# A streaming layer-scale kernel: x's 4 head rows move from the first load to the last, and the tail is cut 56 + 4

## The chip, the cores and the metric

The kernel runs on one core of one Trainium2 chip. The metric is the device time of one execution in microseconds (us), taken as the median of several runs. Smaller is better.

## The reference

The inputs x and y are 1024 x 16 x 512 in bf16, and gamma has 512 elements. The whole computation is one line:

```python
def reference(x, y, gamma):
    return x + gamma * y
```

Flattened, x, y and the output each have 16384 rows of 512 elements, so 1 KB to a row and 16.78 MB to a tensor. Two tensors are read and one is written: 50.33 MB in all, with one multiplication and one addition for each element.

## The kernel before

There is no loop over tiles at run time: four lists, written out by hand at the top of the file, say which transfer and which vector operation is issued in which order.

The 16384 rows are spread over 128 partitions, 128 rows to a partition. `BLOCKS = [4, 64, 60]` cuts them into three blocks of DRAM; inside a block each partition owns consecutive rows. A transfer is written `('y', 4, 68)`: rows 4 to 67 of every partition, 64 rows of 1 KB. This text calls it y64, the first four rows y4, and so on; a store is s64, s4 or s60. `y_sb` holds all 128 rows of y; the products and the sums are written over it in place, and the stores read it. `x_sb` is smaller, 76 rows, and is used twice: the fourth number of an x load is the row of `x_sb` where it lands, so that later loads of x overwrite rows that an addition has already used.

- `SP` (line 12) is what the SyncE queue issues, in order; `ACT` (line 20) is what the ScalarE queue issues: before, it loads x4, then gamma, and then it does all stores. The two queues feed two DMA rings (q1 for SP and q10 for ACT in the profile), and the same 16 DMA engines serve both. Every 128-partition transfer gives each DMA engine 8 partitions; the trace records one packet for each partition of a transfer, and one 4-byte packet for each engine that signals its semaphore.
- `ring` (line 113) issues a list. A load of x waits for the additions whose rows it overwrites (`frees`, line 102). The first `EARLY` transfers of each list are put ahead of everything else in the program. The rest waits (`HOLD`, line 147) until y4 has landed.
- `RELEASE` names the load whose landing lets the stores start. TensorE waits for it (line 157) and then signals ScalarE (`s_go`) and VectorE (`s_rel`).
- `PIECES = [8, 16, 44, 52, 8]` cuts the 128 rows for VectorE; `DVE` lists its work: `('m', c)` multiplies piece c by gamma (line 180), `('a', c)` adds x to it (line 189). A store waits for the additions of the rows it writes.
- gamma arrives as one row, is spread to 128 partitions by a matmul with a row of ones (line 152) and copied to SBUF (line 154).

The order of work around the change, before: SP issues y4 and y64 at once while ACT issues x4; after y4 has landed, SP issues x64 and y60; after the addition of piece 2 it issues x52 (rows 68 to 119), and after the addition of piece 0 it issues x8 (rows 120 to 127). When x52 has landed, the stores go out on ACT's ring: s64, s4, s60.

Of the kernel before, what the change touches and what calls it, by code (L numbers as in the profile page):

```python
# [5 lines left out]

BLOCKS = [4, 64, 60]

PIECES = [8, 16, 44, 52, 8]


SP = [
    ('y', 0, 4),
    ('y', 4, 68),
    ('x', 4, 68, 4),
    ('y', 68, 128),
    ('x', 68, 120, 24),
    ('x', 120, 128, 0),
]
ACT = [('x', 0, 4, 0), ('g',), ('s', 4, 68), ('s', 0, 4), ('s', 68, 128)]  # L20

EARLY = (2, 1)

HOLD, AHEAD = ('y', 0, 4), (2, 1)

RELEASE = ('x', 68, 120, 24)

DVE = [('m', 0), ('m', 1), ('m', 2), ('a', 2), ('a', 0), ('a', 1), ('m', 3), ('m', 4), ('a', 3), ('a', 4)]
MULT, ADD = mybir.AluOpType.mult, mybir.AluOpType.add


def _take(sem, n, eng):


    return eng.wait_ge(sem, n).then_inc(sem, -n)  # L35


def kernel(
# [18 lines left out]
    rows = N // P  # L57
    n = len(PIECES)
    assert sum(PIECES) == rows
    starts = [sum(PIECES[:c]) for c in range(n + 1)]  # L60
    dt = xf.dtype
# [13 lines left out]
    y_sb = nc.alloc_sbuf_tensor("y_sb", [P, rows, D], dt).ap()  # L75
    x_loads = [w for w in ACT + SP if w[0] == "x"]
    y_loads = [w for w in SP + ACT if w[0] == "y"]
    stores = [w for w in SP + ACT if w[0] == "s"]
    for loads in (x_loads, y_loads, stores):
# [9 lines left out]
    s_add, s_go, s_rel, s_end, s_out = sem("s_add"), sem("s_go"), sem("s_rel"), sem("s_end"), sem("s_out")  # L89
    added = [a for kind, *a in DVE if kind == "a"]  # L90
    order = {a[0]: k for k, a in enumerate(added)}

    def meets(a, b, c, d):
        return a < d and c < b
# [4 lines left out]
    def x_at(row):  # L99
        return next(w[3] + row - w[1] for w in x_loads if w[1] <= row < w[2])  # L100
# [12 lines left out]
    def ring(eng, what, n_early, n_ahead):  # L113

        known, went = 0, False
        for k, w in enumerate(what):
            kind = w[0]
            if k == n_ahead:
                _take(s_held[eng], 1, eng)
            need = frees(w) if kind == "x" else pieces_of(w[1], w[2]) + list(w[3:]) if kind == "s" else []  # L120
            need = max((order[c] + 1 for c in need), default=0)
            if kind == "s" and not went:
                _take(s_go, 1, eng)
                went = True
            if need > known:
                eng.wait_ge(s_add, need)
                known = need
            if kind == "g":
                i = eng.dma_start(out=gamma_row, in_=gamma.unsqueeze(0)).then_inc(s_gamma, 16)
            elif kind == "x":  # L130
                to = x_sb[:, w[3] : w[3] + w[2] - w[1], :]
                i = eng.dma_start(out=to, in_=rows_of(xf, w[1], w[2])).then_inc(s_load[w], 16)
            elif kind == "y":
                r = slice(w[1], w[2])
                i = eng.dma_start(out=y_sb[:, r, :], in_=rows_of(yf, w[1], w[2])).then_inc(s_load[w], 16)
            else:
                r = slice(w[1], w[2])
                i = eng.dma_start(out=rows_of(of, w[1], w[2]), in_=y_sb[:, r, :]).then_inc(s_out, 16)
            if k < n_early:
                early.append(i.ins)  # L140

    ring(nc.sync, SP, EARLY[0], AHEAD[0])
    ring(nc.scalar, ACT, EARLY[1], AHEAD[1])

# [11 lines left out]

    _take(s_load[RELEASE], 16, nc.tensor)
    nc.tensor.sem_inc(s_go, 1)
# [4 lines left out]
    def need(loads, c):  # L163
        for w in loads:
            if w not in landed and meets(starts[c], starts[c + 1], w[1], w[2]):
                if w == RELEASE:
                    _take(s_rel, 1, nc.vector)
                elif w == HOLD:
                    _take(s_held[nc.vector], 1, nc.vector)
                else:  # L170
                    _take(s_load[w], 16, nc.vector)
                landed.add(w)

    for kind, *args in DVE:
        c = args[0]
        yt = y_sb[:, starts[c] : starts[c + 1], :]
        if kind == "m":
            need(y_loads, c)
            g = gamma_sb[:, None, :].to_broadcast([P, PIECES[c], D])
            nc.vector.tensor_tensor(out=yt, in0=yt, in1=g, op=MULT).then_inc(s_dve, 1)  # L180
            open_mults += 1
        else:
# [4 lines left out]
            at = x_at(starts[c])  # L187
            xt = x_sb[:, at : at + PIECES[c], :]
            nc.vector.tensor_tensor(out=yt, in0=xt, in1=yt, op=ADD).then_inc(s_add, 1)  # L189
# [44 lines left out]
```

## Time and profile before

| What | Value |
|---|---|
| Time, median of 3 runs | 119.62 us (119.55 to 119.73) |
| Span of the profiled execution, first to last instruction | 118.2 us |
| Time outside the span (median less span) | 1.4 us |
| DMA traffic | 50.33 MB, 1442 packets, mean 426 GB/s |
| DMA rings: share of the time of 16 engines | q1 64.8%, q10 33.9% |
| VectorE busy | 70.1 us, 12 instructions |
| TensorE busy | 0.6 us, one matmul |

The profile states the span of its execution but no separate time for it, so the span is set beside the median of the timed runs. The two shares of the DMA rings add up to 98.7% of the span: the sixteen DMA engines carry packets almost from the first instruction to the last. VectorE's work is spread over 59% of the span. The profile page gives for each DMA issue its size and its time to landing, for instance 57.3 us for y60, which is issued early and waits behind other transfers in its ring.

### The profile page before, as it was taken

To read this page: it belongs to the slowest core of one execution; us is meant where nothing else is said; L and a number is where in the kernel's file an instruction comes from. 1 tells how busy PE (TensorE), PEld (TensorE's weight loads), DVE (VectorE), ACT (ScalarE), POOL (GpSimd) and SP (SyncE) were. 2 spreads that over 40 slices of the span, in tenths; PEclk is the share of its full clock that TensorE was granted. 3 is DMA by queue.
4 is the path that set the end of the run, shared out by engine and by line. 5 is a ranking of instruction groups with operands and counts; after the bars stand their busy time and mean duration, and the time that the engine had idled before them with its cause. 6 is when DMAs were issued, how large, how long until landed. Compare 5 with 4: busy or idle time off the path is not lost. (4 is left out here: it accounts for less than half of the span.)

```text
span 118.2 us, 91 instructions
## 1 busy us (share of the span) xinstructions
PE 0.6 (0%) x1; PEld 0.1 (0%) x1; DVE 70.1 (59%) x12; POOL 0.2 (0%) x4
## 2 busy tenths in 40 slices
PE   0000100000000000000000000000000000000000
PEld 0000000000000000000000000000000000000000
DVE  0000200089999969999999999999999900000000
POOL 0000000000000000000000000000000000000000
DMA  6999889988899879879969696898899889799793
GB/s 248 461 666 399 355 355 399 665 355 355 355 599 466 355 333 624 374 333 499 499 288 576 288 576 288 360 637 355 355 576 488 355 355 510 333 582 416 333 499 166
DMA packets 1442, 50.33 MB, mean 426 GB/s; under 512 B 161, under 2 KB 162, under 8 KB 546
## 3 DMA queue, kind: packets, MB, share of 16 engines
q1 hardware_dynamic: 864, 33.03, 64.8%
q10 hardware_dynamic: 578, 17.30, 33.9%
HBM read 33.56 MB, written 16.78 MB: 426 GB/s over the span
## 5 line engine op out<-in xcount | busy, mean ns | idle before, releaser
L180 DVE TENSOR_TENSOR y_sb<-y_sb,gamma_sb 128x4096 bf16<-128x4096 bf16 (+3 forms) x5 | 34.7, 6981 | 10.9 <-DVEq L35 10.9
L189 DVE TENSOR_TENSOR y_sb<-x_sb,y_sb 128x4096 bf16<-128x4096 bf16 (+3 forms) x5 | 34.7, 6981 | 1.2 <-DVEq L35 1.1
L154 DVE CAST gamma_sb<-gamma_ps 128x512 bf16<-128x512 f32 x1 | 0.7, 692 | 10.2 <-DVEq L35 10.2
L146 DVE MEMSET ones_row<- 1x128 bf16 x1 | 0.2, 165 | 2.0 <-PEq L51 2.0
L152 PE MATMUL gamma_ps<-gamma_row,ones_row 1*128 1x512 bf16 x1 | 0.6, 581 | 11.6 <-PEq L35 11.6
L152 PEld LDWEIGHTS gamma_ps<-gamma_row,ones_row 1*128 1x128 bf16 x1 | 0.1, 101 | 11.6 <-issue 11.6
L218 POOL MEMSET const-bfloat16-1.0<- 128x1 bf16 x1 | 0.1, 101 | 0.0
L218 POOL MEMSET const-uint8-127<- 128x1 uint8 x1 | 0.1, 101 | 0.0
L218 POOL MEMSET const-float32-0.0<- 128x1 f32 x1 | 0.1, 98 | 0.2 <-issue 0.2
L218 POOL MEMSET const-float32-1.0<- 128x1 f32 x1 | 0.1, 98 | 0.0
## 6 DMA issues: line engine op xcount, KB each, us to landing
y_sb<-in_y_dram SPq DMA_DIRECT2D x1, 7680.0 KB, 57.3
out_dram<-y_sb ACTq DMA_DIRECT2D x1, 7680.0 KB, 23.8
x_sb<-in_x_dram SPq DMA_DIRECT2D x1, 6656.0 KB, 21.7
x_sb<-in_x_dram SPq DMA_DIRECT2D x1, 1024.0 KB, 22.0
y_sb<-in_y_dram SPq DMA_DIRECT2D x1, 512.0 KB, 3.4
x_sb<-in_x_dram ACTq DMA_DIRECT2D x1, 512.0 KB, 4.2
out_dram<-y_sb ACTq DMA_DIRECT2D x1, 512.0 KB, 22.3
y_sb<-in_y_dram SPq DMA_DIRECT2D x1, 23.4
```

The lines of the kernel that those rows point to most:

```text
L146: nc.vector.memset(ones_row, 1.0).then_inc(s_ones, 1)
L152: nc.tensor.matmul(gamma_ps, ones_row, gamma_row, start=True, stop=True).then_inc(s_ps, 1)
L154: nc.vector.tensor_copy(out=gamma_sb, in_=gamma_ps).then_inc(s_dve, 1)
L180: nc.vector.tensor_tensor(out=yt, in0=yt, in1=g, op=MULT).then_inc(s_dve, 1)
L189: nc.vector.tensor_tensor(out=yt, in0=xt, in1=yt, op=ADD).then_inc(s_add, 1)
L218: nc = _bacc.Bacc("TRN2", target_bir_lowering=False, num_devices=1)
```

## The change

x4 leaves the head of ACT's list and becomes the last load on SP's ring, so that y64 directly follows y4 there, and ACT starts with gamma. The last 60 rows of x come as 56 and 4 instead of 52 and 8, and the 56-row part is now the `RELEASE`. The pieces follow: 4, 16, 48, 56, 4 rows. The additions are reordered, so that piece 0 (the four head rows) comes last, and its store s4 is now the last store. The rows of `x_sb` are assigned anew: x64 lands at 0, x56 at 16, the last four rows at 72 and x4 at 0.

```diff
-PIECES = [8, 16, 44, 52, 8]
+PIECES = [4, 16, 48, 56, 4]
 SP = [
     ('y', 0, 4),
     ('y', 4, 68),
-    ('x', 4, 68, 4),
+    ('x', 4, 68, 0),
     ('y', 68, 128),
-    ('x', 68, 120, 24),
-    ('x', 120, 128, 0),
+    ('x', 68, 124, 16),
+    ('x', 124, 128, 72),
+    ('x', 0, 4, 0),
 ]
-ACT = [('x', 0, 4, 0), ('g',), ('s', 4, 68), ('s', 0, 4), ('s', 68, 128)]
-EARLY = (2, 1)
-HOLD, AHEAD = ('y', 0, 4), (2, 1)
-RELEASE = ('x', 68, 120, 24)
-DVE = [('m', 0), ('m', 1), ('m', 2), ('a', 2), ('a', 0), ('a', 1), ('m', 3), ('m', 4), ('a', 3), ('a', 4)]
+ACT = [('g',), ('s', 4, 68), ('s', 68, 128), ('s', 0, 4)]
+EARLY = (2, 0)
+HOLD, AHEAD = ('y', 0, 4), (2, 0)
+RELEASE = ('x', 68, 124, 16)
+DVE = [('m', 0), ('m', 1), ('m', 2), ('a', 2), ('a', 1), ('m', 3), ('m', 4), ('a', 3), ('a', 4), ('a', 0)]
```

## The prediction

> **What bounds the kernel now.** I read the page first: the span, the 40 slices and the two DMA rings.
>
> ```profile
> span 118.2 us, 91 instructions
> ...
> DVE  0000200089999969999999999999999900000000
> ...
> DMA  6999889988899879879969696898899889799793
> ...
> DMA packets 1442, 50.33 MB, mean 426 GB/s; under 512 B 161, under 2 KB 162, under 8 KB 546
> ...
> q1 hardware_dynamic: 864, 33.03, 64.8%
> q10 hardware_dynamic: 578, 17.30, 33.9%
> ```
>
> The rings' shares sum to 98.7% of 16 engines' span, 116.7 us. VectorE is idle in the last fifth. So the sixteen DMA engines are the bound; the chain of waits says little here, as it covers only 14% of the span ("issue" 11%, VectorE 3%). The lower digits (6, 7) come from booking a long packet to the slice in which it starts. Whether there are holes is told by single packets. In the trace's packet records, one packet (all of one partition's rows of one transfer) takes 2.418 us for 64 rows, 2.267 for 60, 1.966 for 52, 0.309 for 8 and 0.159 for 4. Every engine has 8 packets of each transfer; following the records engine by engine, each packet starts where the one before ends (overlapping by 3 to 4 ns). The sum per engine: y4, x4, s4: 24 x 0.159 = 3.82; y64, x64, s64: 24 x 2.418 = 58.03; y60, s60: 16 x 2.267 = 36.27; x52: 8 x 1.966 = 15.73; x8: 8 x 0.309 = 2.47. Total 116.32 us. The first packet starts at 1.00 us, the last ends at 117.85, the last store's semaphore lands at 118.19, the span ends at 118.23. So the span is 1.0 us of start, a gapless 116.8, and 0.4 of end. The timed median is 119.62, 1.39 above the span; I take that as constant.
>
> So the change can matter in three ways only: more time in packets, a hole in the stream, or another start or end. For holes I looked at the stretches at the start (columns: stretch, its length, busy time and count of PE, PEld, DVE, POOL, clock, DMA share, GB/s):
>
> ```profile
> 0.00:1.00 1.00, 0.00 (x0) 0.00 (x0) 0.00 (x0) 0.20 (x4) 1.00 0.00 0
> 1.00:1.40 0.40, 0.00 (x0) 0.00 (x0) 0.00 (x0) 0.00 (x0) 1.00 0.79 266
> 1.40:2.20 0.80, 0.00 (x0) 0.00 (x0) 0.17 (x1) 0.00 (x0) 1.00 0.99 389
> 2.20:2.70 0.50, 0.00 (x0) 0.00 (x0) 0.00 (x0) 0.00 (x0) 1.00 1.06 418
> 2.70:3.60 0.90, 0.00 (x0) 0.00 (x0) 0.00 (x0) 0.00 (x0) 1.00 1.01 414
> ```
>
> From 1.4 us all engines are full. Then the rings' packets from 0 to 2.2 us, and from 0 to 3.65:
>
> ```profile
> q1 hardware_dynamic: 102, 0.42, 50.1%
> ```
>
> ```profile
> q1 hardware_dynamic: 144, 0.52, 37.5%
> q10 hardware_dynamic: 122, 0.50, 33.6%
> ```
>
> Up to 2.2 us there is only y4. By 3.65 us q1 has carried 144 = 128 packets of y4 and 16 semaphores, and not one of y64; x4 on q10 has filled the engines meanwhile. That is the point of the change: x4 is a cover between y4 and y64, and it is taken away. Last, the timeline, for VectorE and the issues:
>
> ```profile
> 0.00 0.85 SPq L135 DMA_DIRECT2D y_sb<-in_y_dram  x2
> 0.13 0.38 ACTq L132 DMA_DIRECT2D x_sb<-in_x_dram  x1
> ...
> 43.45 18.43 DVE L189 TENSOR_TENSOR y_sb<-x_sb,y_sb 128x22528 bf16<-128x22528 bf16 x3 [1.08 <-DVEq L35]
> 55.37 2.53 SPq L132 DMA_DIRECT2D x_sb<-in_x_dram  x2
> 61.80 16.22 DVE L180 TENSOR_TENSOR y_sb<-y_sb,gamma_sb 128x26624 bf16<-128x26624 bf16 x2
> 77.41 17.36 ACTq L138 DMA_DIRECT2D out_dram<-y_sb  x3
> ```
>
> **The packets.** The number of transfers stays at ten. x52 and x8 become x56 and a second x4. A 56-row packet isn't in the trace; midway between 52 and 60 rows it is 2.117. Removed: 8 x (1.966 + 0.309) = 18.20; added: 8 x (2.117 + 0.159) = 18.21. That is +0.01 us, nothing. The Trainium skill ("DMA: Bandwidth & Descriptors", Rules for kernel authors) asks for at least 1 MiB per transfer, which speaks against cutting x8's 1 MiB to 0.5. [...]
>
> **The start.** SP's first issue (0.00) and the first packet of y4 (1.00) stay. Without x4 in between, y4's 8 packets on an engine end 1.3 us after its first: at 2.32 on the first engine, 2.73 on the last (engines start between 1.0 and 1.4). y64 is issued at 0.42, its issue takes 0.42 and ends at 0.85. When is it ready? Rows for issue to first packet: y4 on SP 1.00; s64 on ACT at most 1.32 (77.41 to 78.73, behind loads); x4 on ACT 2.08 (0.13 to 2.21); y64 itself at most 3.23 (0.42 to 3.65, behind x4). By the first two y64 is ready at 1.42 to 1.74, with no hole. By x4's row it is 2.51, a hole of 0.18. By its own row it is 3.65, a hole of 1.3. I take the reading that fits all four: transfers issued together become ready one after the other, about 1.2 to 1.4 us apart (1.00, 2.21, 3.65), whichever ring they are on, and a lone one needs 1.0 to 1.3. Then y64 steps into x4's place as the second, ready at 2.21 to 2.44, and the hole is 0 to 0.12; I take 0.05. What speaks for it: a lone ACT issue took at most 1.32, so x4's 2.08 has to be queueing behind y4. The skill (same page, Latency and other measured facts) gives about 0.6 us to the first byte: y4's 0.63 after its issue's end agrees, x4's 1.71 does not. By it alone y64 would be ready at 1.45 and the hole zero.
>
> A first packet on a ring is slow: x4's cost 0.02 us per engine over its 0.159s; that goes. Net of the start: +0.03.
>
> **The middle.** y4 lands some 0.3 earlier (3.38 now), so x64 (3.71) and gamma (3.90) go out about 0.3 earlier; both ends of that wait are hidden behind y64's 19 us. All loads after y4 run 1.27 earlier (8 x 0.159). VectorE's prices by elements: 4096 take 2.29, 8192 4.42, 22528 11.89, 26624 14.02, so 2048 take 1.22, 24576 12.95, 28672 15.09. x64 lands at 42.2 (43.45 less 1.27); m1 and m2 end at about 40.1 and aren't in the way. a2 then ends at 55.1, and x56 is issued there, not at 55.37; its ring has y60 until 59.4 (60.66 now), so 4.2 us of cover are left of 5.3. x4 waits for a1 (59.6), with x56 ahead in the ring until 76.3. m3 starts when y60 has landed (60.1) and with m4 ends at 76.4, before the release. Without this cover each us late would cost one, but over 4 are left.
>
> **The release and the stores.** Before the release one engine carries x56 in place of x52 and x4: -0.06, so it stays at about 77.3 and the first store at 77.4. s64 needs at most 1.32 to its first packet; the loads left behind are 16 x 0.159 = 2.5 us, as x8's 8 x 0.309 = 2.5. If s64 is ready sooner, packets of x4 alternate with its 2.4 us packets and x4 lands later, by some 10 us for four packets, at about 89. a0, which needs it, comes after a3 (77.4 + 15.1 = 92.5) and a4 (93.7), so it is covered by 4 us. s60 is issued at 93.8 (94.43 now), s64 has the ring until 98.0 at the earliest. s4 is issued at 95.0 behind s60's 18 us. The last semaphore lands 0.36 after its packet now; for s4, whose landing is no later behind its packet than s64's in this trace, I take the same.
>
> **Sum.** +0.01 +0.03 = +0.04, so 119.66; I give 119.65. About 0.2% (0.24 us) is what a measurement of this kernel can tell from no change.
>
> **The rivals.**
> - *y64 isn't ready when y4 ends (slower).* If y64's lateness doesn't come from x4 but from its own ring (it follows y4's semaphore packets, 2.71 to 3.05, by 0.94), the hole is 0.94 after y4's end; if it is its own issue's latency, 1.3. Nothing hides a hole, as the engines are never idle later: 120.5 to 120.9. It decides once y64 is ready after 2.6 us or so. For it: the rings alternated packet by packet while both y4 and x4 had some, but y64 never alternated with x4's last five or six, so it was ready only at about 3.3 or later. Against it: x4 waited too, on another ring. 0.28.
> - *The start gets cleaner (faster).* The packets of the first 15 us carry 0.24 us per engine over their usual times (0.09 y4, 0.02 x4, 0.13 y64). If two rings starting together cause them, and the engines' spread of 0.44 at the end shrinks with them, 0.25 to 0.35 is gained: 119.3. The spread is there before x4's first packet, which speaks against it. 0.10.
> - *The change moves the cover but not the time.* That is the forecast: the engines carry the same bytes with no hole, 119.5 to 119.85. 0.62. VectorE or the release becoming late would need over 4 us and has next to nothing.
>
> **How the numbers follow.** The likeliest case gives 119.65, with 119.45 to 119.85 from its hole of 0 to 0.18 and the spread of runs (0.1 either way). The range goes up to 120.55, the near end of the slower rival, of which about half lies beyond, and down to 119.4. Faster 0.10, same 0.62, slower 0.28.
>
> **What would show it.** Right: the 2.2 to 2.7 and 2.7 to 3.6 stretches still show a DMA share near 1 (or more, where a 2.4 us packet starts), y64's first packet at about 2.3 to 2.7, x64's addition at about 42.2, the stores' first issue at 77.4, and the last store's end at 117.9. Wrong: no packets between 2.7 and 3.6, with everything after y4 later by that hole, the first store at 78.3 or later; or a hole where s64 follows the loads (78.7 to 79.2); or s60 issued after 98.

## The result, and the profile after

The changed kernel took 120.0 us in the median of 12 runs (119.76 to 120.07), the kernel before 119.69 (119.55 to 119.94) in 12: a ratio of 1.0017, with a 95% interval of 1.0009 to 1.0025. Two further sets of runs gave 1.0013 (1.0004 to 1.0022) and 1.0002 (0.9990 to 1.0014), with medians 119.85 against 119.79 and 119.83 against 119.77. So the change costs between nothing and 0.3 us, most likely 0.1 to 0.2. The forecast was 119.65, no change within 0.24 us, with 0.62 on it.

The page of the kernel after shows the same picture as before, a span 0.5 us longer and the same bytes, with more of them on q1:

```profile
span 118.7 us, 91 instructions
...
DMA  9888998889888997797797997898898889979974
...
DMA packets 1442, 50.33 MB, mean 424 GB/s; under 512 B 161, under 2 KB 162, under 8 KB 674
...
q1 hardware_dynamic: 1008, 33.55, 65.9%
q10 hardware_dynamic: 434, 16.78, 32.7%
```

98.6% of the sixteen engines' span is packets, against 98.7% before. Next the start, in the same stretches as before (stretch, length, busy time and count of PE, PEld, DVE, POOL, clock, DMA share, GB/s):

```profile
1.00:1.40 0.40, 0.00 (x0) 0.00 (x0) 0.00 (x0) 0.00 (x0) 1.00 0.81 174
1.40:2.20 0.80, 0.00 (x0) 0.00 (x0) 0.17 (x1) 0.00 (x0) 1.00 0.96 369
2.20:2.70 0.50, 0.00 (x0) 0.00 (x0) 0.00 (x0) 0.00 (x0) 1.00 3.57 1491
2.70:3.60 0.90, 0.00 (x0) 0.00 (x0) 0.00 (x0) 0.00 (x0) 1.00 1.22 514
```

The share of 3.57 is y64's packets: the view books 2.4 us of each to the stretch it starts in. The ring's packets from 0 to 3.65 us say the same:

```profile
q1 hardware_dynamic: 160, 1.57, 108.7%
```

160 are the 128 packets of y4, 16 semaphores, and now 16 of y64, one for each engine. In the packet records they start between 2.56 and 2.96 us, each within 6 ns of the packet before it: no hole. The timeline:

```profile
0.00 0.84 SPq L136 DMA_DIRECT2D y_sb<-in_y_dram  x2
...
3.70 0.33 SPq L133 DMA_DIRECT2D x_sb<-in_x_dram  x1
...
42.41 17.30 DVE L190 TENSOR_TENSOR y_sb<-x_sb,y_sb 128x24576 bf16<-128x24576 bf16 x2 [2.28 <-DVEq L36]
55.40 4.66 SPq L133 DMA_DIRECT2D x_sb<-in_x_dram  x3
60.47 16.23 DVE L181 TENSOR_TENSOR y_sb<-y_sb,gamma_sb 128x28672 bf16<-128x28672 bf16 x2 [0.76 <-DVEq L36]
77.86 18.17 ACTq L139 DMA_DIRECT2D out_dram<-y_sb  x3
```

x64's addition starts 1.04 us earlier than before, x56 is issued at about the same time, and the stores start at 77.86 instead of 77.41. VectorE waits for loads in two new places, 0.76 us before the multiplication at 60.47 and 1.46 before the addition at 78.15; neither holds up a transfer, as s60 is issued at 94.41 us (94.43 before), while s64's packets are still running.

**Where the time went in this pair of traces.** Taking the mean over the sixteen engines, I cut the stream at the first packet of y64, the first of s64, and the last semaphore packet. Where x4's eight packets lie in a stretch, 1.25 us is taken off (8 x 0.1555 + 0.0055, the records' steps). The table adds those traces of the experiments below in which loads and stores keep the order and sizes of one of the two kernels; "order only" has before's loads.

| Kernel, trace | to y64's first | y64's first to s64's first | s64's first to the end |
|---|---|---|---|
| before, 1 | 2.54 | 75.12 | 38.68 |
| before, 2 | 2.84 | 75.09 | 38.69 |
| before, 3 | 2.74 | 75.10 | 38.68 |
| order only | 2.74 | 75.10 | 38.69 |
| after, 1 | 2.68 | 75.31 | 38.68 |
| after, 2 | 2.74 | 75.20 | 38.69 |
| after, 3 | 2.71 | 75.12 | 38.69 |

The first trace of before had the shortest start, so part of the 0.34 us between the two first traces (117.93 against 117.59 at the end, on the mean of the engines) is chance. Over all traces the start costs the same, 2.72 before and 2.71 after. The stores cost the same to 0.01 us, with s4 last or in the middle. What is left is the middle, where single packets, scattered over the loads, ran long: 75.31 and 75.20, but 75.12 in the third trace, whose set of runs is also the one with the ratio 1.0002.

### The profile page after: what moved, and what is told of

Same layout as the page of the kernel before. It is cut to its first block, busy times and chain, and to the rows that moved or that the text cites. A ratio compares the mean times of both kernels' runs of the same rounds, so it can differ in the third digit from the quotient of the medians.

```text
span 118.7 us, 91 instructions
## 1 busy us (share of the span) xinstructions
PE 0.6 (0%) x1; PEld 0.1 (0%) x1; DVE 70.3 (59%) x12; POOL 0.2 (0%) x4
## 5 line engine op out<-in xcount | busy, mean ns | idle before, releaser
L181 DVE TENSOR_TENSOR y_sb<-y_sb,gamma_sb 128x2048 bf16<-128x2048 bf16 (+3 forms) x5 | 34.7, 6982 | 8.1 <-DVEq L36 8.1
L190 DVE TENSOR_TENSOR y_sb<-x_sb,y_sb 128x2048 bf16<-128x2048 bf16 (+3 forms) x5 | 34.7, 6981 | 3.7 <-DVEq L36 3.7
```

## The experiments

**The two kernels again**, unchanged, for the scatter of traces and times.

> The kernel before, once more, as a measure of what a second trace and a second set of times of the same kernel differ by. All theories: ratio 1.000 within 0.001. The start theory (the lost time sits before y64's first packets, as a slower run of y4's packets): all 16 engines busy by 1.4 us again, and y64's first packets at 3.79 us on the mean of the engines, within 0.04. The slow-packet theory (the lost time is single packets that run long in the middle of the loads, by chance): between the first packet of y64 and that of s64 this trace has 75.1 us again, or up to 0.2 us more if chance does it for any kernel.

> The changed kernel, once more. All theories: ratio 1.001 to 1.0025. Start theory: the engines are again not all busy until 1.6 us, and y64's first packets come at 2.68 us on the mean, which is 0.14 us later than before less the eight 4-row packets of x4. Slow-packet theory by chance: the stretch from y64's first packet to s64's is nearer to its packets' sum of 76.16 us than the 76.56 of the first trace. If both are the same as in the first trace, the slow packets belong to the change.

Measured: before, 119.80 us, ratio 1.0003 (0.9994 to 1.0011); after, 119.85 us, 1.0013 (1.0004 to 1.0022). The expectation of the start failed: before's own y64 came at 4.09 instead of 3.79 us, as y4's packets ran long by 0.3 us per engine more. That is as large as anything seen in the changed kernel's start, so the start theory fell here. The stretch in the middle, 75.09 for before and 75.20 for after, left the slow-packet theory open.

**The tail alone, and the move alone.**

```diff
 # tail alone, against before
-PIECES = [8, 16, 44, 52, 8]
+PIECES = [4, 16, 48, 56, 4]
-    ('x', 68, 120, 24),
-    ('x', 120, 128, 0),
+    ('x', 68, 124, 20),
+    ('x', 124, 128, 0),
-RELEASE = ('x', 68, 120, 24)
+RELEASE = ('x', 68, 124, 20)
 # move alone, against after
-PIECES = [4, 16, 48, 56, 4]
+PIECES = [4, 16, 48, 52, 8]
-    ('x', 68, 124, 16),
-    ('x', 124, 128, 72),
+    ('x', 68, 120, 16),
+    ('x', 120, 128, 68),
-RELEASE = ('x', 68, 124, 16)
+RELEASE = ('x', 68, 120, 16)
```

> The tail alone: x's last 60 rows come as 56 and 4, pieces 4, 16, 48, 56, 4; x4 stays at the head of the other ring and the stores keep their order. Start theory: same as before, ratio 1.000 within 0.0007, y64's first packets at 3.79 us. Rival, the tail costs (smaller packets ahead of the stores, or a later release): 1.0015 to 1.002, with a hole or long packets where s64 follows the loads near 79 us.

> The move alone: x4 is the last load and s4 the last store, but the tail stays 52 and 8 rows. Start theory: as the changed kernel, ratio 1.001 to 1.0025, y64's first packets at 2.68 us. Rival, the tail costs: same as before, 1.000 within 0.0007.

Measured: the tail alone 120.49 us, 1.0065 (1.0050 to 1.0080); the move alone 120.58 us, 1.0069 (1.0056 to 1.0082). Each part costs 0.7 to 0.8 us by itself, and together they cost 0.1 to 0.2. No theory of mine had that. The stretches of the tail alone show the first half of the reason:

```profile
78.50:79.00 0.50, 0.00 (x0) 0.00 (x0) 0.00 (x0) 0.00 (x0) 1.00 0.97 393
79.00:79.40 0.40, 0.00 (x0) 0.00 (x0) 0.20 (x1) 0.00 (x0) 1.00 0.12 41
79.40:79.80 0.40, 0.00 (x0) 0.00 (x0) 0.40 (x1) 0.00 (x0) 1.00 0.78 328
```

Between 79.0 and 79.8 the engines stand still: 0.74 us on the mean of the engines in the records. The stores' packets start at 79.79, the share of 0.78 being the first to be booked. The steps of that wait, from the trace: x56's last packet ends at 78.16, its semaphore is complete at 78.56, the first store is issued at 78.91, its first packet starts at 79.79. That is 1.63 us after the last packet of the release's load; and the fastest engine has passed that point some 0.4 us sooner. Only x's last four rows, 1.25 us, lie in between. In the changed kernel x4 stands behind them as well, 2.5 us, and there the engines have no hole at the joint (the place where the stores follow the loads). So x4 at the end is the cover that the 56 + 4 tail needs.

The move alone has no such hole at the joint (0.2 us of idle time in all from 76 to 80 us). It releases the stores with 3.7 us of loads left, 12 rows, and its loads' packets ran long. The next experiment asked which.

**The move alone, with its last two loads swapped**, so that the larger packets come last.

```diff
 # against the move alone
     ('x', 68, 120, 16),
-    ('x', 120, 128, 68),
     ('x', 0, 4, 0),
+    ('x', 120, 128, 68),
```

> The move alone (tail 52 and 8, release by x52), but with the last two loads swapped: x4, then x8. The stores are still released 3.7 us before the loads end. If that early release itself costs (stores being started while loads run): 1.006 to 1.007 again, with long packets of x8 at 78 to 79 us. If only 4 KB packets suffer from it: 1.000 to 1.002.

Measured: 120.31 us, 1.0036 (1.0023 to 1.0049), between the two expectations, with long packets of x8. The view of stretches shows the loads' rate after an early release (x8 last, first fence) and in the changed kernel (second fence):

```profile
77.50:78.50 1.00, 0.00 (x0) 0.00 (x0) 1.00 (x1) 0.00 (x0) 1.00 1.15 360
78.50:79.00 0.50, 0.00 (x0) 0.00 (x0) 0.50 (x1) 0.00 (x0) 1.00 0.73 262
```

```profile
77.50:78.50 1.00, 0.00 (x0) 0.00 (x0) 0.35 (x1) 0.00 (x0) 1.00 1.02 418
78.50:79.00 0.50, 0.00 (x0) 0.00 (x0) 0.50 (x1) 0.00 (x0) 1.00 1.03 426
```

Both stretches hold loads only, as no store packet starts before 79.07 in either. The first store is issued at 76.45 in the first kernel and at 77.86 in the second. In the first, x8's packets of 0.309 us take up to 0.72, from 77.46 on, 1.0 us after that issue; together 0.36 us per engine. In the move alone it was x4's and a few of x8's, from 77.72 on, 0.36 us as well, and 0.2 us of holes. So in both kernels with an early release, loads that still run well after the stores' issue take longer, before a store packet is recorded. Most of the long packets start late: of the load packets that start 1.6 to 2.4 us after the stores' issue, 18 of 27 run over 0.03 us long with x8 last and 21 of 48 in the move alone, but of those that start 1.0 to 1.6 us after it only 6 of 32 and 1 of 33. In the three traces of after, the three of before and the one of the order alone, 203 load packets start 1.0 to 1.6 us after the issue, none of them long, and only five start later. VectorE's next addition starts with the release too, but its additions from 43 to 62 us in the first trace of before ran beside loads that lost 0.02 us per engine. That the issue of the stores is the cause is read from this timing; no run changed it alone, and how it would work no run here shows. What the runs do show, of three places for the release: 1.25 us of loads behind it are too few, 3.7 us are too many, and before and after both have 2.5.

**A head of two rows**, to measure when y64 is ready.

```diff
 # against after (slots of x_sb, PIECES and stores follow)
-BLOCKS = [4, 64, 60]
+BLOCKS = [2, 64, 62]
-PIECES = [4, 16, 48, 56, 4]
+PIECES = [2, 16, 48, 58, 4]
-HOLD, AHEAD = ('y', 0, 4), (2, 0)
+HOLD, AHEAD = ('y', 0, 2), (2, 0)
```

> The changed kernel with a head of 2 rows instead of 4 (blocks 2, 64, 62; x's tail 58, 4 and 2), so that y's head lasts only some 0.7 us on an engine and ends at about 1.7 to 2.1 us. It measures when y64 is ready as the second transfer of its ring. One-after-the-other theory (the prediction's): ready at 2.2 to 2.45, so y64's first packets leave a hole of 0.2 to 0.6 us after y2's. Lone-latency theory (ready 1.0 to 1.3 after its issue, at 1.4 to 1.75): no hole, y64's first packets at 1.7 to 2.1. Own-ring rival (0.94 after the head's semaphore packet): a hole of 0.9 us.

Measured: 120.25 us, 1.0044 (1.0024 to 1.0064), with times from 119.88 us upwards; the profiled execution is one of the longer, 121.61 with a span of 120.3, so what its trace shows need not be the usual run. The ring's packets from 0 to 1.75 and from 0 to 2.3 us:

```profile
q1 hardware_dynamic: 130, 0.57, 91.2%
```

```profile
q1 hardware_dynamic: 158, 1.18, 142.1%
```

By 2.3 us, 158 packets have started: 128 of y2, 16 semaphores and 14 of y64. The first of y64's starts at 1.677 us, 6 ns after its engine's semaphore packet. So on that engine it was ready at most 1.25 us after its issue (0.42), which is the row of a lone issue: the one-after-the-other theory (2.2 us or later) is refuted, and so is the own-ring rival (0.94 us after the semaphore). But two engines got their first y64 packet only at 3.10 and 3.47, after holes of 1.2 and 1.6 us. They stayed that late for the whole load phase, the release waited for them, and at the joint the other engines had run dry: 1.37 us of idle time on the mean, between 79 and 81 us. Part of it is a shorter cover: x's last four rows and its two head rows are 2.0 us, not 2.5. A four-row head lasted until 2.36 us or later, and where y64 follows it on the ring, no trace had such a hole.

**x4 on SP's ring between y4 and y64; the order of the stores alone; x4 in the middle.** The counts in `EARLY` and `AHEAD`, not shown, follow the lists: three early issues on SP in the first, two in the third, none on ACT.

```diff
 # one ring, against before
     ('y', 0, 4),
+    ('x', 0, 4, 0),
     ('y', 4, 68),
-ACT = [('x', 0, 4, 0), ('g',), ('s', 4, 68), ('s', 0, 4), ('s', 68, 128)]
+ACT = [('g',), ('s', 4, 68), ('s', 0, 4), ('s', 68, 128)]
 # order only, against before
-ACT = [('x', 0, 4, 0), ('g',), ('s', 4, 68), ('s', 0, 4), ('s', 68, 128)]
+ACT = [('x', 0, 4, 0), ('g',), ('s', 4, 68), ('s', 68, 128), ('s', 0, 4)]
 # x4 in the middle, against before
     ('x', 4, 68, 4),
+    ('x', 0, 4, 0),
     ('y', 68, 128),
-ACT = [('x', 0, 4, 0), ('g',), ('s', 4, 68), ('s', 0, 4), ('s', 68, 128)]
+ACT = [('g',), ('s', 4, 68), ('s', 0, 4), ('s', 68, 128)]
```

> The kernel before, with x4 as the second load of SP's ring instead of the first of ACT's: y4, x4, y64 on one ring, three early issues. If only a cover of small packets matters and not the ring: same as before, 1.000 within 0.001, y64's first packets at 3.8 to 4.1 us on the mean. If a second ring at the start is what fills the engines: all 16 busy only at 1.6 us, and 1.001 to 1.002.

> The kernel before with the stores in the order s64, s60, s4, as in the changed kernel. Theory of the start and of long load packets: same as before, 1.000 within 0.001, and the store stretch is again its packets' sum of 38.67 us. Rival, the short store at the end costs: 1.001 to 1.002, seen as a later last landing or a wider spread of the engines' ends.

> The kernel before, with x4 moved only to the middle: it goes on SP's ring between x64 and y60, the head is y4 and y64 on one ring as in the changed kernel, the tail and the stores are those of before. If y64 needs no cover at the start: 1.000 to 1.001, no hole near 2.5 us. If the change's 0.2 us comes from the head: 1.0015 to 1.002. If from the tail of 16 small packets: 1.000.

Measured: one ring 120.71 us, 1.0088 (1.0075 to 1.0101), a miss: y64's first packets, 2.57 to 3.67 us long instead of 2.418 (0.48 us per engine more), a hole of 0.2 us before them and one of 0.14 at the joint. Why the same two small loads cost nothing on two rings and 1 us on one was not found. Order only: 119.75 us, 1.0003 (0.9995 to 1.0012), so a short store at the end is free. x4 in the middle: 119.88 us, 1.0002 (0.9989 to 1.0015), with no hole at 2.7 us: y64 right after y4 on one ring is free too.

**y64 first**, so that no small packet opens the stream. Gamma and x64 no longer wait for y4, and VectorE multiplies piece 0 third (`DVE`, not shown).

```diff
 # against after
 SP = [
-    ('y', 0, 4),
     ('y', 4, 68),
+    ('y', 0, 4),
-EARLY = (2, 0)
-HOLD, AHEAD = ('y', 0, 4), (2, 0)
+EARLY = (2, 1)
+HOLD, AHEAD = ('y', 0, 4), (3, 1)
```

> [...] If the start's loss is 4 KB packets that run long while further transfers are being started (0.3 to 0.6 us in the four traces so far): faster than the changed kernel by 0.2 to 0.4 us, ratio to before 0.998 to 1.000. If the loss is in the engines' staggered start alone: as the changed kernel, 1.001 to 1.002.

Measured: 120.38 us, 1.0061 (1.0049 to 1.0072), the opposite of what was expected. The first y64 packets took 2.75 to 3.35 us, 0.68 us per engine more than usual. So it isn't the 4 KB packets alone that make the start slow. How much longer than 2.418 us the first packets of 64 rows ran differs by kernel: 0.0 to 0.4 us where they follow a four-row y4 on the ring (2.4 to 3.0 us), 0.2 to 0.8 in the two-row head (1.7 to 3.5 us), 0.3 to 0.9 here (1.0 to 1.5), but 0.2 to 1.3 with x4 between them on one ring (3.6 to 4.6). So coming early is not what decides it, and the cause stays open.

**The third pair of traces.**

> The kernel before, a further trace, for one question: do the long packets in the middle of the loads belong to the change? From the first packet of y64 to that of s64 the three traces with x4 at the head, 64-row transfers undisturbed and x8 as cover took 75.09 to 75.12 us on the mean of the engines. If the long packets belong to the change: again 75.05 to 75.15. If they come by chance to any kernel: this can be up to 75.4.

> The changed kernel, a third trace. The same stretch less x4's eight packets (1.25 us) took 75.31 and 75.20 us in its first two traces. If the long packets belong to the change: 75.2 to 75.35 again, and a ratio of 1.001 to 1.0025. If by chance: it can be 75.1.

Measured: before 119.77 us, 0.9995 (0.9982 to 1.0008), middle stretch 75.10; after 119.83 us, 1.0002 (0.9990 to 1.0014), middle stretch 75.12. The changed kernel can run its loads as smoothly as the one before. Four traces with before's loads had 75.09 to 75.12, though, three of after 75.12 to 75.31, and x4 in the middle, whose ratio is 1.0002, 75.36. Whether the long packets come somewhat more often when x4 is not at the head, or by chance alone, these runs do not settle.

## Why the prediction was right

- **No hole before y64**: right, and shown, but hit by luck, as the step's reasoning failed. "Transfers issued together become ready one after the other, about 1.2 to 1.4 us apart" is wrong: with a two-row head y64 was ready on the first engine at 1.68 us. The row of the lone issue, which gave "no hole", was about right for 14 engines (1.68 to 2.22 us); the other two were over 1 us later, which no row of before showed.
- **y4 lands 0.3 us earlier**: not in this pair. x64 was issued at 3.70 (3.71 before). y4's last semaphore packet came at 2.95 (3.05 before) instead of about 2.7, as its packets ran 0.21 us per engine over (0.09 before). Over the other traces x64 was issued at 3.62 and 3.58 in after, at 3.97 and 3.82 in before, so the step was right on the mean. Either way it cost nothing, being hidden as said.
- **The middle**: right in its order and covers. x64's addition at 42.41 (42.2 forecast), x56 issued at 55.40 (55.1), the third multiplication at 60.47 (60.1). The term missing from the sum is the long packets, 0.0 to 0.2 us by trace; the sum took them as equal to before's.
- **The release and the stores**: the first store's issue was put at 77.4 and came at 77.86, as the late start and middle were passed on (77.56 and 77.53 in the other two traces); the joint had no hole, as forecast. The alternation of x4's packets with s64's, named as a possibility, did not come: even in the move alone, with 3.7 us of loads behind the release, s64 began on each engine only when the loads had ended. The tail was priced by its packets, +0.01 us, and that holds only because x4 comes to stand behind it: the prediction counted the same 2.5 us on both sides, but did not say that the tail alone would lose that cover (0.74 us of idle engines, shown).
- **The rivals**: the slower one, with a hole of 0.94 us or more, is refuted by the changed kernel's own start, and its two reasons by the 6 ns of the two-row head, though two engines there had holes of that size. The cleaner start did not show either: the start is 2.72 us on the mean of four traces and 2.71 of three.
- **The size**: +0.04 us forecast, about +0.1 to +0.2 measured, inside the 0.24 that was called no change. The first set alone, 120.0 us, lies above the 119.85 of the likeliest case.

## What to carry to other kernels

When DMA engines are never idle, moving a transfer can be free if every joint keeps its cover (x4 in the middle cost nothing), so price the joints as well as the transfers: count from the last packet of the load that releases the next phase, on its slowest engine, to the first packet of what it releases (1.6 us here, plus 0.4 of spread), and leave that much queued behind it, but not much more. That count does not see everything: x4 as the second load of SP's ring cost 1 us, about half of it in long packets. Two edits that each cost 0.7 us can together cost 0.1, so test the parts before dropping one. And one trace of a kernel is one draw: its start varied by 0.3 us between traces of the same kernel, as much as the effect that was looked for.

## What was not expected of the hardware

- Loads that still ran after the stores' issue slowed down in two kernels before any store packet appeared: 0.309 us packets took up to 0.72, most of them 1.6 to 2.4 us after the issue.
- The first packets of 64 rows took 2.75 to 3.35 us instead of 2.418 when they opened the stream at 1.0 us.
- A late engine stays late: two engines 1.2 to 1.6 us late at the start of the two-row head came back, with a shorter cover, as 1.37 us of idle time on the mean 77 us later.
